# Attention scores in bursts of four blocks, with the high x high products as pairs of 64-row matmuls

## The chip, the cores and the metric

The kernel runs on one core of a Trainium2 chip. The metric is the device time of one execution, in microseconds; of the kernel before it is 1637.64 us, the median of three runs (1636.85 to 1638.16). A smaller time is better.

## What is computed

Attention without a softmax, followed by two layers of a mixture of experts. Cut to what the change touches:

```python
# B, S, D = 4, 3072, 256; d_qk = 64; inputs fp32, drawn from a normal distribution times 0.1
scores = (1 / S) * np.matmul(z, z.transpose(0, 2, 1))     # z: 4 x 3072 x 64
attn = np.maximum(scores, 0.0) ** 2
out = u * np.matmul(attn, v)                              # u, v: 4 x 3072 x 256
# then out.reshape(12288, 256) goes through two layers of 8 experts with 1024 hidden units,
# the first with a capacity of 1536 tokens an expert, the second with 384
```

## The kernel before

Products are made to nearly fp32 exactness out of fp32r matmuls: each operand is split into a high part (a copy in fp32r) and a low part (what is left), and a product is a sum of partial products of highs and lows.

Attention takes the 4 batches in chunks of 512 queries: 6 chunks a batch, 24 in all (`c`, of `NC`). For each chunk it goes through the 24 blocks of 128 keys (`k`, of `KT`); a step `s` is one block of one chunk, 576 in all (`NS`). What a step makes is transposed: keys on partitions, queries on columns.

- `load_z`, `part_z`, `turn_z` bring a tile of 512 rows of z and turn it, so that its 64 features stand on partitions, twice: rows 0 to 63 and again 64 to 127. `turn_z` makes `zHL`: the high part in the upper 64 rows, the low part in the lower. `swap_z` makes `zLH` for one chunk, the same with halves exchanged, by two DMAs from POOL's queue.
- `scores(s)` (lines 363 to 382) makes one block: the first matmul (L368) takes 128 columns of `zHL` as weights and the chunk's `zHL` as moving operand, which gives high x high + low x low; the second (L369) takes the same weights and `zLH`, for the two mixed terms. Both use all 128 rows of the array and 512 columns. ScalarE applies Relu and the scale (L371, `r`). The square `a` is made by VectorE (L379) or ScalarE (L377), its high part `aH` by ScalarE (L376, L380), its low part `aL` by VectorE (L382).
- `av(s)` multiplies with v: for each half `h` of the 256 columns of v three matmuls (L397 to L399) of 128 rows and 512 columns add to the accumulator `accs[h]`, through all 24 blocks. At the last block VectorE multiplies with the turned u (L401, `times_u` in the change) into `xT`.

The order on every queue is that in which the program text issues (nothing is rescheduled). `scores` runs three steps ahead of `av` (`LA`), so TensorE's stream is: two score matmuls of step s + 3, six matmuls of step s, and so on. What else belongs to a chunk hangs on steps as hooks (`at(step, function, ...)`), issued after that step: loading and turning u (`turn_u`, steps 12 and 16 of a chunk), `swap_z` for the next chunk (step 13), and for the chunk before it the gate's logits (`part_x`, `logits`, `turn_l`, `put_l`) and the output (`put_x` at step 9, which for the first ten chunks turns `xT` into `rowb` and issues eight DMAs). In the chunk that ends a batch, and a little ahead, z and v of the next batch are split (`turn_z`, `part_v`). During the last batch the routing of the first expert layer (`prep`, `prep2`) is worked off between the steps. Behind attention come the experts, in `fast`, with 384 to 432 columns a matmul or 256.

PSUM has eight banks: three `acc`, two `sc`, and one each of `mi`, `rt` and `px`.

## Time and profile before

| | |
|---|---|
| median of the runs | 1637.64 us |
| the profiled execution | 1636.56 us, its span 1634.8 us |
| TensorE busy | 1580.8 us, 97% |
| VectorE busy | 1186.5 us, 73% |
| ScalarE busy | 1116.7 us, 68% |
| granted TensorE clock, mean | 0.983 of full speed |
| attention's matmuls | 7.4 to about 1105 us |

Engines are named as in the trace: PE is TensorE, PEld its weight loads, DVE is VectorE, ACT is ScalarE, POOL is GpSimd, SP issues DMAs. A row of a matmul shows 0.39 us for 512 columns although the next one starts 0.23 us later: matmuls are pipelined, and a row contains its way through the array. So lengths of a stream of matmuls are read from their starts. "Issue" as the reason of a gap means that the profile shows nothing that the engine waited for.

### The profile page before, as it was taken

Reading aid. Unit: us, or ns where it says so; the run is one execution under the profiler, and the core shown is the slowest. Engines: PE = TensorE matmul, PEld = TensorE weight load, DVE = VectorE, ACT = ScalarE, POOL = GpSimd, SP = SyncE. Lnnn points to the kernel's source line nnn. Section 1 sums busy time; section 2 is a strip of 40 time slices with the busy share of each in tenths; the row PEclk is TensorE's granted clock in tenths of the full one; section 3 lists DMA queues with packets and bytes.
Section 4 is the critical chain, followed back from the end, with each engine's and each line's share of the span. In section 5 each row is a group of like instructions: output and inputs, shape, how many; then the busy total and the mean of one; then the engine's idle time right before and its main releaser. Section 6 shows DMA issues by size and latency. Waiting matters only on the chain.

```text
span 1634.8 us, 24914 instructions
## 1 busy us (share of the span) xinstructions
PE 1580.8 (97%) x8570; PEld 1326.7 (81%) x8570; DVE 1186.5 (73%) x2338; ACT 1116.7 (68%) x1937; POOL 333.1 (20%) x518
## 2 busy tenths in 40 slices
PE   8999999999999999999999999999999969989997
PEld 5888887888888888888887777878888759978997
DVE  6877788777778767777877877677777766775652
ACT  7877788777788877778987767884444316644552
POOL 1000000000000000000000478642333113323341
PEclk9999999999999999999999999999999969999999
DMA  6111355322335212224310112223343204644540
GB/s 136 20 27 33 68 136 133 73 70 76 72 67 130 76 46 59 59 66 86 77 33 21 28 20 45 60 80 118 101 124 103 84 19 134 189 134 124 153 129 28
DMA packets 282681, 132.44 MB, mean 81 GB/s; under 512 B 216717, under 2 KB 268173, under 8 KB 282544
## 3 DMA queue, kind: packets, MB, share of 16 engines
q1 hardware_dynamic: 269264, 106.90, 26.0%
q0 software_dynamic: 13280, 23.85, 5.0%
q8 instruction: 69, 1.13, 0.3%
q14 instruction: 68, 0.56, 0.1%
HBM read 84.61 MB, written 40.55 MB: 77 GB/s over the span
## 4 chain that ended last, share of the span: by engine, by line
PE 70%; issue 16%; DVE 7%; POOL 2%; ACT 2%; DMA 1%; SPq 1%; POOLq 0%; DVEq 0%
PE acc L397 12%; PE acc L398 12%; PE acc L399 12%; PE sc L1013 9%; PE sc L368 6%; PE sc L369 6%; PE acc L1163 5%; PE mi L1114 2%; DVE pL L225 1%; PE rt L866 1%; PE mi L336 1%; PE acc L1320 1%; PE acc L1321 1%; PE acc L1322 1%; DVE hL L1023 1%
## 5 line engine op out<-in xcount | busy, mean ns | idle before, releaser
L382 DVE TENSOR_TENSOR aL<-a,aH 128x512 fp32r<-128x512 f32 x576 | 398.6, 693 | 212.9 <-ACT a L377 157.8
L371 ACT ACTIVATE r<-sc 128x512 f32<-128x512 f32 x576 | 343.0, 595 | 186.6 <-PE sc L369 180.7
L397 PE MATMUL acc<-aH,pH 128*128 128x512 f32 x1152 | 449.7, 390 | 0.0
L398 PE MATMUL acc<-aL,pH 128*128 128x512 f32 x1152 | 449.0, 390 | 0.0
L399 PE MATMUL acc<-aH,pL 128*128 128x512 f32 x1152 | 448.5, 389 | 0.0
L379 DVE TENSOR_TENSOR a<-r 128x512 f32<-128x512 f32 x344 | 238.5, 693 | 43.0 <-ACT r L371 41.8
L397 PEld LDWEIGHTS acc<-aH,pH 128*128 128x128 f32 x1152 | 216.7, 188 | 45.6
L399 PEld LDWEIGHTS acc<-aH,pL 128*128 128x128 f32 x1152 | 216.7, 188 | 45.6
L398 PEld LDWEIGHTS acc<-aL,pH 128*128 128x128 f32 x1152 | 216.7, 188 | 45.5
L368 PE MATMUL sc<-zHL 128*128 128x512 f32 x576 | 229.8, 399 | 6.3 <-DVE zHL L280 6.0
L1021 ACT ACTIVATE hH<-sc 128x432 fp32r<-128x432 f32 (+2 forms) x192 | 90.0, 469 | 212.5 <-PE sc L1013 208.2
L369 PE MATMUL sc<-zLH,zHL 128*128 128x512 f32 x576 | 225.3, 391 | 0.2 <-DVE zLH L284 0.2
L380 ACT ACTIVATE aH<-r 128x512 fp32r<-128x512 f32 x344 | 217.8, 633 | 10.9
L347 POOL TENSOR_TENSOR lgs<-lgb 32x128 f32<-32x128 f32 x23 | 15.2, 659 | 853.2 <-DVE lgb L344 853.2
L376 ACT ACTIVATE aH<-r 128x512 fp32r<-128x512 f32 x232 | 146.7, 632 | 7.4
L1023 DVE SCALAR_TENSOR_TENSOR hL<-sc,hH 128x432 fp32r<-128x432 f32 (+2 forms) x192 | 99.3, 523 | 65.6 <-ACT hH L1021 65.4
L377 ACT ACTIVATE a<-r 128x512 f32<-128x512 f32 x232 | 142.8, 616 | 0.0
L368 PEld LDWEIGHTS sc<-zHL 128*128 128x128 f32 x576 | 108.7, 189 | 36.1 <-DVE zHL L280 7.4
L1013 PE MATMUL sc<-xTH,pH 128*128 128x384 f32 (+2 forms) x368 | 125.9, 342 | 5.9 <-DVE hL L1023 5.8
L369 PEld LDWEIGHTS sc<-zLH,zHL 128*128 128x128 f32 x576 | 108.8, 189 | 21.5 <-DVE zLH L284 0.5
L1013 PE MATMUL sc<-xTL,pH 128*128 128x384 f32 (+2 forms) x368 | 120.0, 326 | 0.0
L1013 PE MATMUL sc<-xTH,pL 128*128 128x384 f32 (+2 forms) x368 | 119.8, 326 | 0.0
(333 smaller groups left out, 2261.4 us busy)
## 6 DMA issues: line engine op xcount, KB each, us to landing
raw<-in_moe_w_dram SPq DMA_DIRECT2D x84, 512.0 KB, 3.7
raw<-in_v_dram SPq DMA_DIRECT2D x24, 512.0 KB, 4.3
uraw<-in_u_dram SPq DMA_DIRECT2D x192, 64.0 KB, 2.3
out_dram<-zt SPq DMA_DIRECT2D x24, 512.0 KB, 4.2
xb<-xT SPq DMA_DIRECT2D x14, 512.0 KB, 3.4
zr<-in_z_dram SPq DMA_DIRECT2D x96, 64.0 KB, 2.4
zLH<-zHL POOLq DMA_DIRECT2D x46, 128.0 KB, 2.3
ya<-zt SPq DMA_DIRECT2D x10, 544.0 KB, 3.5
```

Of the source, the lines that this page charges most:

```text
L368: nc.tensor.matmul(p, lw, zHL[b, c % QC], start=True, stop=False)
L369: nc.tensor.matmul(p, lw, zLH[c], start=False, stop=True)
L371: nc.scalar.activation(r, p, AF.Relu, scale=SCALE)
L376: nc.scalar.activation(HS[s], r, AF.Square)
L377: nc.scalar.activation(a, r, AF.Square)
L379: nc.vector.tensor_tensor(a, r, r, OP.mult)
L380: nc.scalar.activation(HS[s], r, AF.Square)
L382: nc.vector.tensor_tensor(LS[s], a, HS[s].bitcast(F32), OP.subtract)
L397: nc.tensor.matmul(accs[h], vh[sl], HS[s], start=k == 0, stop=False)
L398: nc.tensor.matmul(accs[h], vh[sl], LS[s], start=False, stop=False)
L399: nc.tensor.matmul(accs[h], vl[sl], HS[s], start=False, stop=k == KT - 1)
L1013: nc.tensor.matmul(p, a, b[:, d, :w], start=i == 0, stop=i == 5)
```

## The change

- Tiles of z are kept in a new form, `zK`: in columns 0 to 255 the high part is in the upper 64 rows and the low part in the lower, in columns 256 to 511 the other way round. For the current chunk there are whole tiles `zHL` and `zLH`. `swap_z` and `copy_z` make these from `zK`: the half columns that stand the right way round are copied by ScalarE, the others exchanged by four DMAs from POOL's queue instead of two.
- `burst(s)` makes the scores of four blocks at once into four banks. First four matmuls of 64 rows for the high x high terms, in the order block 0, 2, 1, 3, of which the first and third use the upper 64 rows of the array (tile position 0) and the second and fourth the lower (tile position 64). Then one matmul of 128 rows a block for both mixed terms. The product low x low is no longer made.
- A burst is issued at the first step of a group of four, for the group after it; `squares` spreads its Relus and squares over the four steps of the group. ScalarE squares for `a` in one or two blocks of four, where before it was every second or every third block.
- `av` takes one half at a time, with the low part of the square in the third matmul instead of the second. In a chunk's last four blocks, the last three are done first for half 0, then for half 1, so that `times_u` of half 0 stands ahead of the matmuls of half 1. At a chunk's first step the burst stands between the halves.
- PSUM in attention: two `acc`, four `sc`, one `mi`, one `rt`, no `px`; after attention a new pool with the layout of before (`open_psum`). The routing's table `tabh` goes to `rt`.
- SBUF: `rowb` shares the one buffer of `uT`, `lgb` the two of `zT`; `r` has three buffers. The constant `idr` is dropped. In the start `turn_z` of the second z tile stands ahead of the first steps.

```diff
...
-        self.ps = pool("ps", 1, space=PSUM)
+        self.nacc, self.nsc = 2, 4
...
-        return self.ps.tile([128, 512], F32, name=name, tag="acc", bufs=3)
+        return self.ps.tile([128, 512], F32, name=name, tag="acc", bufs=self.nacc)
...
-        return self.ps.tile([128, 512], F32, name=name, tag="sc", bufs=2)
+        return self.ps.tile([128, 512], F32, name=name, tag="sc", bufs=self.nsc)
...
-        o = pool.tile([128, 2, 512], F32, name="rowb", bufs=1)
+        o = pool.tile([128, 2, 512], F32, name="rowb", tag="uT", bufs=1)
...
-        with self.tc.tile_pool(name="attn", bufs=2) as W:
+        with self.tc.tile_pool(name="attn", bufs=2) as W, \
+                self.tc.tile_pool(name="psa", bufs=1, space=PSUM) as self.ps:
             return self._attention(W, *args)
+    def open_psum(self):
+        self.ps = self.ctx.enter_context(self.tc.tile_pool(name="ps", bufs=1, space=PSUM))
+        self.nacc, self.nsc = 3, 2
...
+        def parts_z(t, z, o, a, b):
+            nc.vector.tensor_tensor(t[o:o + 64, a:b], z[o:o + 64, a:b], t[o:o + 64, a:b].bitcast(F32), OP.subtract)
...
-            t = zHL[b, i] = W.tile([128, 512], FR, name="zHL", bufs=QC + 2)
-            first = b == i == 0
+            t = zK[b, i] = W.tile([128, 512], FR, name="zK", bufs=QC + 2)
             nc.scalar.activation(t, zT[b, i], AF.Copy)
-            nc.vector.tensor_tensor(t[64:128], zT[b, i][64:128], t[64:128].bitcast(F32), OP.subtract)
-            if first:
-                l = zLH[0] = W.tile([128, 512], FR, name="zLH", bufs=2)
-                nc.scalar.activation(l, zT[b, i], AF.Copy)
-                nc.vector.tensor_tensor(l[0:64], zT[b, i][0:64], l[0:64].bitcast(F32), OP.subtract)
+            if b == i == 0:
+                zHL[0] = W.tile([128, 512], FR, name="zHL", bufs=2)
+                nc.scalar.activation(zHL[0], zT[b, i], AF.Copy)
+                zLH[0] = W.tile([128, 512], FR, name="zLH", bufs=2)
+                nc.scalar.activation(zLH[0], zT[b, i], AF.Copy)
+            parts_z(t, zT[b, i], 64, 0, 256)
+            if b == i == 0:
+                parts_z(zLH[0], zT[b, i], 0, 0, 512)
+            parts_z(t, zT[b, i], 0, 256, 512)
+            if b == i == 0:
+                parts_z(zHL[0], zT[b, i], 64, 0, 512)
...
             b, q = divmod(c, QC)
-            t = W.tile([128, 512], FR, name="zLH", bufs=2)
-            s = zHL[b, q]
-            nc.gpsimd.dma_start(t[0:64], s[64:128])
-            nc.gpsimd.dma_start(t[64:128], s[0:64])
-            zLH[c] = t
+            s = zK[b, q]
+            h = zHL[c] = W.tile([128, 512], FR, name="zHL", bufs=2)
+            l = zLH[c] = W.tile([128, 512], FR, name="zLH", bufs=2)
+            for t, a in ((l, 0), (h, 256)):
+                for o in (0, 64):
+                    nc.gpsimd.dma_start(t[o:o + 64, a:a + 256], s[64 - o:128 - o, a:a + 256])
+        def copy_z(c, d):
+            b, q = divmod(c, QC)
+            t, a = ((zHL[c], 0), (zLH[c], 256))[d]
+            nc.scalar.activation(t[:, a:a + 256], zK[b, q][:, a:a + 256], AF.Copy)
...
-                uT[c] = W.tile([128, 2, 512], F32, name="uT", bufs=1)
+                uT[c] = W.tile([128, 2, 512], F32, name="uT", tag="uT", bufs=1)
...
-                b = W.tile([32, 512], F32, name="lgb", bufs=1)
+                b = W.tile([128, 512], F32, name="lgb", tag="zT", bufs=2)[:32]
...
-        HS, LS = {}, {}
-        LA = 3
-        def scores(s):
+        HS, LS, R = {}, {}, {}
+        GB = 4
+        accs = None
+        def burst(s):
             c, k = divmod(s, KT)
-            b = c // QC
-            p = self.sc()
-            lw = zHL[b, k // 4][:, k % 4 * 128:(k % 4 + 1) * 128]
-            nc.tensor.matmul(p, lw, zHL[b, c % QC], start=True, stop=False)
-            nc.tensor.matmul(p, lw, zLH[c], start=False, stop=True)
-            r = W.tile([128, 512], F32, name="r", bufs=2)
-            nc.scalar.activation(r, p, AF.Relu, scale=SCALE)
+            K = zK[c // QC, k // 4]
+            P = [self.sc() for _ in range(GB)]
+            cols = [slice(j * 128, (j + 1) * 128) for j in range(GB)]
+            for j in (0, 1):
+                nc.tensor.matmul(P[j], K[0:64, cols[j]], zHL[c][0:64], start=True, stop=False, tile_position=(0, 0))
+                nc.tensor.matmul(P[j + 2], K[64:128, cols[j + 2]], zLH[c][64:128], start=True, stop=False,
+                                 tile_position=(64, 0))
+            for j in range(GB):
+                nc.tensor.matmul(P[j], K[:, cols[j]], (zLH if j < 2 else zHL)[c], start=False, stop=True)
+            return P
+        def relu(s, p):
+            R[s] = W.tile([128, 512], F32, name="r", bufs=3)
+            nc.scalar.activation(R[s], p, AF.Relu, scale=SCALE)
+        def square(s, act):
+            r = R.pop(s)
             a = W.tile([128, 512], F32, name="a", bufs=2)
-            HS[s] = W.tile([128, 512], FR, name="aH", bufs=LA + 1)
...
-            if k % (2 if c == 0 or c % QC == QC - 1 or b == B - 1 else 3) == 1:
-                nc.scalar.activation(HS[s], r, AF.Square)
+            h = HS[s] = W.tile([128, 512], FR, name="aH", bufs=GB)
+            if not act:
+                nc.vector.tensor_tensor(a, r, r, OP.mult)
+            nc.scalar.activation(h, r, AF.Square)
+            if act:
                 nc.scalar.activation(a, r, AF.Square)
-            else:
-                nc.vector.tensor_tensor(a, r, r, OP.mult)
-                nc.scalar.activation(HS[s], r, AF.Square)
-            LS[s] = W.tile([128, 512], FR, name="aL", bufs=LA + 1)
-            nc.vector.tensor_tensor(LS[s], a, HS[s].bitcast(F32), OP.subtract)
-        accs = None
-        def av(s):
+            LS[s] = W.tile([128, 512], FR, name="aL", bufs=GB)
+            nc.vector.tensor_tensor(LS[s], a, h.bitcast(F32), OP.subtract)
...
+        def squares(s, j, P):
+            c, k = divmod(s, KT)
+            if j == 0:
+                relu(s, P[0])
+            if j < 3:
+                relu(s + j + 1, P[j + 1])
+            busy = c == 0 or c % QC == QC - 1 or c // QC == B - 1
+            square(s + j, j == 1 or j == 3 and (busy or k // GB % 2 == 1))
+        def av(s, h):
+            c, k = divmod(s, KT)
+            vh, vl = V[c // QC, k // 4]
+            sl = (slice(None), k % 4, slice(h * 128, (h + 1) * 128))
+            nc.tensor.matmul(accs[h], vh[sl], HS[s], start=k == 0, stop=False)
+            nc.tensor.matmul(accs[h], vl[sl], HS[s], start=False, stop=False)
+            nc.tensor.matmul(accs[h], vh[sl], LS[s], start=False, stop=k == KT - 1)
+        def times_u(c, h):
+            nc.vector.tensor_tensor(xT[c][:, h], accs[h], uT[c][:, h], OP.mult)
+        def step(s):
             nonlocal accs
             c, k = divmod(s, KT)
-            b = c // QC
+            j = k % GB
+            g = s - j + GB
+            last = k >= KT - GB
             if k == 0:
                 accs = [self.acc(), self.acc()]
-            vh, vl = V[b, k // 4]
-            if k == KT - 1:
                 xT[c] = self.w.tile([128, 2, 512], F32, name="xT", bufs=1)
-            for h in range(2):
-                sl = (slice(None), k % 4, slice(h * 128, (h + 1) * 128))
-                nc.tensor.matmul(accs[h], vh[sl], HS[s], start=k == 0, stop=False)
-                nc.tensor.matmul(accs[h], vh[sl], LS[s], start=False, stop=False)
-                nc.tensor.matmul(accs[h], vl[sl], HS[s], start=False, stop=k == KT - 1)
-                if k == KT - 1:
-                    nc.vector.tensor_tensor(xT[c][:, h], accs[h], uT[c][:, h], OP.mult)
-                    if h == 0 and s + LA < NS:
-                        scores(s + LA)
+            if j == 0:
+                av(s, 0)
+                if k > 0:
+                    av(s, 1)
+                if g < NS:
+                    PS[0] = burst(g)
+                if k == 0:
+                    av(s, 1)
+            elif last and j == 1:
+                for i in range(3):
+                    av(s + i, 0)
+                times_u(c, 0)
+                for i in range(3):
+                    av(s + i, 1)
+            elif not last:
+                av(s, 0)
+                av(s, 1)
+            if g < NS:
+                squares(g, j, PS[0])
+            if last and j == 1:
+                times_u(c, 1)
...
-        part_v(0, 0)
-        part_z(0, 1)
...
-            at(4 * i - 4 - d, turn_z, 0, i)
             if i > 1:
+                at(4 * i - 5 - d, turn_z, 0, i)
                 at(4 * i - 6 - d, part_z, 0, i)
...
                 at(s0 + 17, load_u, c + 1)
-                at(s0 + 13, swap_z, c + 1)
+                at(s0 + 11, swap_z, c + 1)
+                at(s0 + 13, copy_z, c + 1, 0)
+                at(s0 + 15, copy_z, c + 1, 1)
...
-        for s in range(LA):
-            scores(s)
+        PS[0] = burst(0)
+        squares(0, 0, PS[0])
+        part_v(0, 0)
+        for j in range(1, GB):
+            squares(0, j, PS[0])
+            if j == 1:
+                part_z(0, 1)
+                turn_z(0, 1)
         for s in range(NS):
-            if s + LA < NS and s % KT != KT - 1:
-                scores(s + LA)
-            av(s)
...
-        px = self.px("tabh")
+        px = self.rt("tabh")
...
+        m.open_psum()
         fast(ctx, tc, m, moe_w1, moe_w2, moe2_w1, moe2_w2, out, W, rows)
...
```

## Rows read from the trace of the kernel before

**Rows 1.** The page, engines: busy us, share of the span, instructions.
```profile
PE 1580.8 (97%) x8570; PEld 1326.7 (81%) x8570; DVE 1186.5 (73%) x2338; ACT 1116.7 (68%) x1937; POOL 333.1 (20%) x518
```
**Rows 2.** Stretches: length, busy PE, PEld, DVE, ACT, POOL, clock, DMA share, GB/s.
```profile
300.00:400.00 100.00, 100.00 (x443) 82.09 (x442) 73.86 (x112) 77.93 (x132) 4.53 (x9) 1.00 0.33 79
```
**Rows 3.** Waits of PE, whole run: us in total, times, longest.
```profile
PE sc L368 <- DVE zHL L280: 6.0, 3, 2.7
```
**Rows 4.** Timeline of PE in attention: start us, duration us, engine, line, operation.
```profile
600.29 0.39 PE L369 MATMUL sc<-zLH,zHL 128*128 128x512 f32 x1
...
602.34 0.39 PE L368 MATMUL sc<-zHL 128*128 128x512 f32 x1
...
604.16 0.39 PE L368 MATMUL sc<-zHL 128*128 128x512 f32 x1
```
**Rows 5.** Timeline of PE in the experts, around an 8-row matmul.
```profile
1132.58 0.35 PE L1013 MATMUL sc<-xTL,pH 128*128 128x432 f32 x1
1132.87 0.18 PE L871 MATMUL rt<-gO,ones 8*128 8x32 bf16 x1
1132.98 0.46 PE L1163 MATMUL acc<-hH,pH 128*128 128x432 f32 x1
1133.28 0.36 PE L1163 MATMUL acc<-hL,pH 128*128 128x432 f32 x1
1133.48 0.36 PE L1163 MATMUL acc<-hH,pL 128*128 128x432 f32 x1
```
**Rows 6.** Timeline of PEld there; in brackets the idle time before and why.
```profile
1132.86 0.09 PEld L871 LDWEIGHTS <-ones 8*128 8x128 bf16 x1 [0.28 <-issue]
...
1133.28 0.19 PEld L1163 LDWEIGHTS acc<-hH,pL 128*128 128x128 f32 x1
```
**Rows 7.** Groups by form, PEld: busy us, mean ns | idle before, releaser.
```profile
L984 PEld LDWEIGHTS mi<-idf,g 48*128 48x128 f32 x16 | 2.2, 135 | 2.7 <-issue 2.7
```
**Rows 8.** Timeline of PEld, four 16-row loads in a stream of full ones.
```profile
1113.72 0.32 PEld L352 LDWEIGHTS mi<-idf,lgT 16*128 16x128 f32 x4 [0.29 <-issue]
```
**Rows 9.** Timeline of ACT in attention.
```profile
599.53 0.63 ACT L376 ACTIVATE aH<-r 128x512 fp32r<-128x512 f32 x1
600.08 0.62 ACT L377 ACTIVATE a<-r 128x512 f32<-128x512 f32 x1
600.72 0.60 ACT L371 ACTIVATE r<-sc 128x512 f32<-128x512 f32 x1
601.35 0.63 ACT L380 ACTIVATE aH<-r 128x512 fp32r<-128x512 f32 x1
```
**Rows 10.** Stretches: an ordinary chunk, and one that prepares a batch.
```profile
152.20:196.70 44.50, 44.50 (x197) 36.48 (x196) 32.52 (x51) 34.70 (x59) 1.51 (x3) 1.00 0.30 63
...
241.30:286.70 45.40, 45.16 (x197) 36.04 (x196) 39.32 (x59) 40.85 (x71) 1.97 (x3) 1.00 0.57 140
```
**Rows 11.** Groups by form, ACT, 241.3 to 286.7 us.
```profile
L234 ACT ACTIVATE pH<-raw 128x1024 fp32r<-128x1024 f32 x4 | 4.2, 1046 | 0.0
L279 ACT ACTIVATE zHL<-zT 128x512 fp32r<-128x512 f32 x4 | 2.5, 630 | 2.7 <-DVE zT L273 2.7
```
**Rows 12.** Timeline of DVE, second chunk: `rowb` and the next `uT`.
```profile
81.69 1.30 DVE L195 STREAM_TRANSPOSE rowb<-xT 128x512 f32<-128x512 f32 x2
...
87.13 0.70 DVE L315 STREAM_TRANSPOSE uT<-uraw 128x512 f32<-128x512 f32 x1
```
**Rows 13.** Timeline of SP's queue there.
```profile
82.42 4.18 SPq L199 DMA_DIRECT2D xa<-rowb  x8
```
**Rows 14.** The page, DMA issues: count, KB each, us from issue to landing.
```profile
zLH<-zHL POOLq DMA_DIRECT2D x46, 128.0 KB, 2.3
...
xa<-rowb SPq DMA_DIRECT2D x80, 64.0 KB, 1.9
```
**Rows 15.** Timeline of POOL in the last batch.
```profile
1042.31 0.58 POOL L290 DMA_DIRECT2D zLH<-zHL  x1
```
**Rows 16.** The page, groups: busy us, mean ns | idle before, releaser.
```profile
L382 DVE TENSOR_TENSOR aL<-a,aH 128x512 fp32r<-128x512 f32 x576 | 398.6, 693 | 212.9 <-ACT a L377 157.8
```

More of the change, by code (lines that the diff above doesn't have):

```diff
@@ L138, in consts @@
         make_identity(nc, self.idf)
-        self.idr = c.tile([128, 128], FR, name="idr")
-        nc.scalar.activation(self.idr, self.idf, AF.Copy)
         self.wgraw = c.tile([128, 2, 8], F32, name="wgraw")
@@ L257, in _attention @@
         NC = B * QC
-        zr, zT, zHL, vr, V, zLH, uraw, uT, xT, row, xp, lg = ({} for _ in range(12))
+        zr, zT, zK, vr, V, zHL, zLH, uraw, uT, xT, row, xp, lg = ({} for _ in range(13))
         def at(s, f, *a):
@@ L271, in part_z @@
         def part_z(b, i):
-            zT[b, i] = W.tile([128, 512], F32, name="zT", bufs=2)
+            zT[b, i] = W.tile([128, 512], F32, name="zT", tag="zT", bufs=2)
             nc.vector.transpose(zT[b, i], zr[b, i])
+        def parts_z(t, z, o, a, b):
+            nc.vector.tensor_tensor(t[o:o + 64, a:b], z[o:o + 64, a:b], t[o:o + 64, a:b].bitcast(F32), OP.subtract)
         def turn_z(b, i):
-            t = zHL[b, i] = W.tile([128, 512], FR, name="zHL", bufs=QC + 2)
-            first = b == i == 0
+            t = zK[b, i] = W.tile([128, 512], FR, name="zK", bufs=QC + 2)
@@ L405, in put_l @@
+        PS = [None]
         def put_l(c):
@@ L454, in _attention @@
                     at(t + 3, part_v, b + 1, i)
-        for s in range(LA):
-            scores(s)
+        PS[0] = burst(0)
[6 more added lines that the diff above has]
+                turn_z(0, 1)
         for s in range(NS):
-            if s + LA < NS and s % KT != KT - 1:
-                scores(s + LA)
-            av(s)
+            step(s)
             for f, a in hooks.pop(s, []):
```

## The prediction

> **What bounds the kernel now.** I read the page first: TensorE shows 97% of the span busy, the next engine, VectorE, 73% [rows 1]. A busy matmul row overlaps its neighbour, so that share alone proves little; the table by stretches does. In the attention stage, which runs to about 1105 us and holds all that the diff touches but the order of PSUM banks afterwards, TensorE is busy for 100 us of 100, ScalarE for 78 and VectorE for 74, at the granted clock 1.00, 2.4 GHz [rows 2]. The waits of TensorE agree: the longest entry in the whole run is 6.0 us, three waits for the low parts of z in the start [rows 3]. So attention lasts as long as its matmuls follow each other. Their spacing is in the timeline: from the first score matmul of one block to that of the next, eight matmuls of 512 columns, 1.82 us pass, 0.227 us each [rows 4] (a row reads 0.39 us because it overlaps the next). 576 blocks of eight at 0.227 us are 1046 us. What shortens this stream shortens the run; what only moves work off ScalarE or VectorE doesn't, until one of them is late.
>
> **The change on TensorE.** Per four blocks the score part goes from eight full matmuls to four of 64 rows and four full ones; the 24 of the value product stay. The 64-row ones stand in pairs, on row tiles 0 and 64. If a pair takes the time of one, two slots are saved, 2 x 0.227 = 0.454 us a group, and 144 groups give 65 us. That is what the change would bring if nothing else happened.
>
> But the array goes from its full shape to 64-row tiles and back, once each per group, and the trace of before has this step. In the FFN an 8-row matmul (L871) stands in a stream of full ones with 432 columns, spaced 0.195 us (0.20 in the rows, rounded). The full one before it starts at 1132.58; the weight load of the 8-row one starts at 1132.86, 0.28 us later, after 0.28 us of idle that is put down to nothing but "issue" [rows 5, 6]. Ordinarily the next weights start loading when the matmul before starts (1133.28 and 1133.28), hidden under it. Behind the 8-row one the full matmul takes 0.46 us instead of 0.36: its own weights lie open for 0.10 to 0.11 us [rows 5, 6]. From 1132.58 to 1133.28, 0.70 us, stand two matmuls that would take 0.39. The same holds for 48-row fp32 ones, which use a 64-row tile as the change does: 16 of them cost 2.7 us of idle before their weights, 0.17 each, all of it "issue" [rows 7]; and four 16-row ones show 0.29 us [rows 8].
>
> The Trainium skill says the same in general (TensorEngine Tiling (Array Packing), Key Properties): changing the tiling mode, not just the tile, drains TensorE. This speaks against the change, and the trace agrees [rows 5 to 8]; the skill gives no figure, so the sum goes by the rows.
>
> Now the sum for a group, from the start of the last full matmul before the burst to the start of the first full one in it. Before: five slots, 5 x 0.227 = 1.135 us. After: 0.28 us as read, and 0.03 more since 512 columns take 0.227 and not 0.195, is 0.31 until the first weights load; x until the first 64-row product can start; 0.227 for its pair; l, by which the second tile lags the first because its weights come second; 0.31 until the full weights load; 0.11 until their matmul starts. 0.31 + x + 0.227 + l + 0.31 + 0.11 = 0.957 + x + l. No row shows weights of 64 rows in fp32r or two row tiles at once. Weights of 128 rows lie open for 0.11 us [rows 5]; those of 16 rows follow one another in (0.32 - 0.14)/3 = 0.06 us, with 0.14 the length of one load on a small row tile [rows 7, 8]. So x lies in 0.06 to 0.11 and l in 0 (both loaded at once) to 0.11. I take x = 0.11, the row of the same type, and l = 0.085, the middle of the two loads: 1.152 us, 0.017 more than before. 144 groups: +2.4 us; with the bounds, -0.118 to +0.042 a group, -17 to +6 us. The two saved slots just about pay the two changes of shape. If a pair's halves don't overlap at all, a group costs 0.31 + 0.11 + 3 x 0.227 + 0.31 + 0.11 = 1.521, +0.386, +56 us; if changes of shape cost nothing here, -65 us.
>
> **What feeds TensorE.** Scores now come four blocks at once, a group ahead. From the start of the first full score matmul to its Relu 0.43 us pass (600.29 to 600.72 in [rows 4, 9]); then two Relus and a square at 0.63 each [rows 9] and the subtraction at 0.69 [rows 16] give the first aL 2.6 us after. It is needed 4 + 18 + 2 matmuls later, 24 x 0.227 - 0.43 = 5.0 us. Slack: 2.4 us. With two squares more on ScalarE (0.55 after a square, and the next Relu 0.64 after it [rows 9]) a busy group takes it 4 x 0.63 + 2 x 0.63 + 2 x 0.55 + 2 x 0.64 = 6.2 us of 7.3, so in most chunks it idles a tenth of the time or more (34.7 of 44.5 us before [rows 10]; after, one square and two half copies more, some 36).
>
> Only a chunk that prepares the next batch is tight: 40.9 us of 45.4 [rows 10]. There each group also splits one z tile (0.63) and one v tile (1.05) [rows 11], 7.9 us against 7.3; over five groups that is 3 us too much, with part_x (two more copies of 0.63) and the new half copies (two, each between half of 0.63 and the whole) some 5 us, against 2.4 of slack and what idles around. I take 1 us of stall in each of three such chunks, and 1 us in the first chunk, which splits all of batch 0: +4 us, bounds 0 and +12. VectorE has the same work but a few smaller subtractions; its cover is the quarter of its time that is free.
>
> **Waits and queues.** (1) uT and rowb share one buffer. rowb is turned at 81.69 us, its eight stores are issued from 82.42 for 4.18 us and land 1.9 us after each issue, so until about 88; uT is turned at 87.13 [rows 12 to 14]. turn_u will therefore hold VectorE for about 1 us in ten chunks; queued behind it are the next aL and a, on which the value product waits. Their slack is the 2.4 us above, so I cost it at 0; without that cover 10 us. (2) Only two acc banks: the first matmul of a chunk waits for times_u on half 0. That was finished nine matmuls (2.0 us) earlier, more than the 0.69 us of a VectorE operation of this size [rows 16]: 0, or 24 x 0.7 = 17 us without cover. (3) aH has four buffers, and with halves apart the second block's is free only 12 matmuls after the burst, 1 us after ScalarE wants it, once a chunk: covered by its idle time, else 24 us. (4) POOL issues four swap DMAs a chunk instead of two, at 0.6 us each; they are needed nine steps, 16 us, later, and land in 2.3 us [rows 14, 15]: 0 even among the scatters of the last batch, up to 2 us if these come later for it. lgb in zT's buffers, tabh in rt's bank and the new PSUM pool after attention: 0, bound 2 us. (5) Start: TensorE waits 6.0 us in all for z's tiles, 2.7 at the longest [rows 3]. Now three copies and four subtractions stand before the first mixed term, but z's second tile is turned earlier: 0, plus or minus 2.
>
> **Sum.** +2.4 + 4 = +6.4 us on the profiled execution, 1636.6 us (span 1634.8 and 1.8 around it), 1643.0. The median of the runs lies 1.1 above that execution: 1644.1. I forecast 1644, about 0.4% slower: the order of the work is new and its length is not.
>
> **Rivals.**
> *A. The second tile's weights load with the first's, and little stalls* (faster). Then l = 0 and x = 0.06, -0.118 a group, -17 us: 1620.6. Cheaper changes of shape in a stream of long matmuls would take it on towards 1572, where all 65 us stay. For it: 8-row loads are shorter than 128-row ones. Against it: three kinds of rows show the open weights and the drain alike [rows 5 to 8]. It decides as soon as l is under 0.04 and nothing stalls. The Trainium skill bears on this (TensorE: Matmul & The Clock Gate, Part 3, The mechanism): weight loads for another row group may be pulled ahead and matmuls on row tiles start some 4 ns apart. No row here has two tiles at once; by it the time is this rival's.
> *B. The pairs run one after the other.* The change then doesn't do what it says: +56 us, and 4 of stalls, 1697. For it: no row of before shows two at once, and matmuls start in order. Against it: they use different rows and different banks.
> *C. ScalarE becomes the bound in every chunk* through the held aH buffer and the shared uT buffer: some 1.1 us in each of 24 chunks instead of the 4 us, +26 + 2: 1666. For it: batches of four need four Relus at once. Against it: a fifth of ScalarE's time is idle in most chunks [rows 10].
>
> **How the numbers follow.** Forecast (1630 to 1658) 0.55, A 0.25, B 0.10, C 0.10. About 0.2%, 3.3 us, is what a measurement can tell from no change. Of the forecast's 0.55 some 0.08 fall below 1634.4, 0.13 within 3.3 us of 1637.6, 0.34 above. Faster: 0.25 + 0.08 = 0.33; same 0.13; slower 0.34 + 0.10 + 0.10 = 0.54. The range leaves out B and the far end of A: 1612 to 1668.
>
> **What would show it.** In the changed kernel: two idle stretches per group at the weight loads, before the first 64-row one and before the first full one; starts of the two halves of a pair under 0.11 us apart (0.227 apart would be B); 1.13 to 1.18 us from the last full matmul before a burst to the first full one in it (1.02 would be A); waits of TensorE for aL or aH in the chunks that prepare a batch, and hardly elsewhere. The forecast is wrong if the drains are shorter than the rows of L871 and L984, or if TensorE waits in every chunk.

## The result, and the profile after

The changed kernel takes 1655.53 us, the median of four runs (1654.26 to 1657.11), beside 1637.9 us for the kernel before: 1.0108 times as long, with a 95% interval of 1.009 to 1.0125. It is 17.6 us slower where 6.4 were forecast. The profiled execution has a span of 1653.4 us, 18.6 more than before.

The page, engines of the changed kernel (busy us, share of the span, instructions), which answers [rows 1]:

```profile
PE 1584.9 (96%) x8568; PEld 1253.5 (76%) x8570; DVE 1172.1 (71%) x2349; ACT 1056.4 (64%) x1997; POOL 353.4 (21%) x564
```

Hardly anything shows: TensorE is 4 us busier and GpSimd 20, the others are less busy. So I laid the ends of the chunks beside each other: the start of the second multiplication by u of a chunk (L401 before, L433 after, 24 of them, on VectorE's timeline), us.

| end of chunk | before | after | difference |
|---|---|---|---|
| 0 | 63.66 | 62.39 | -1.27 |
| 4 | 241.32 | 240.50 | -0.82 |
| 5 (prepares a batch) | 286.68 | 287.29 | +0.61 |
| 11 | 553.52 | 554.04 | +0.52 |
| 17 | 820.36 | 820.82 | +0.46 |
| 20 | 968.71 | 969.74 | +1.03 |
| 21 | 1017.72 | 1025.86 | +8.14 |
| 23 | 1106.43 | 1119.37 | +12.94 |
| first expert product | 1106.23 | 1120.72 | +14.49 |
| last matmul | 1622.58 | 1637.14 | +14.56 |
| end of the span | 1634.75 | 1653.37 | +18.62 |

Three batches, 18 of 24 chunks, come out even. 12.5 us come in the six chunks of the last batch, 1.5 in the handover to the experts, nothing in the experts, and 4.1 behind the last matmul. The stretches agree (length, busy PE, PEld, DVE, ACT, POOL, clock, DMA share, GB/s): of the changed kernel a chunk that prepares a batch and an ordinary one, which answer [rows 10], and its last batch in two halves; last, the same two halves of the kernel before.

```profile
240.50:287.30 46.80, 46.03 (x198) 33.28 (x196) 40.51 (x64) 39.65 (x75) 2.65 (x5) 1.00 0.63 153
152.20:196.70 44.50, 44.50 (x198) 33.34 (x198) 31.32 (x50) 32.17 (x62) 2.77 (x5) 1.00 0.25 41
...
820.80:969.70 148.90, 145.57 (x761) 106.03 (x760) 109.66 (x206) 101.51 (x193) 43.07 (x72) 0.99 0.14 28
969.70:1119.40 149.70, 142.16 (x626) 103.22 (x624) 100.58 (x203) 101.92 (x190) 93.82 (x157) 0.99 0.21 53
...
820.40:968.70 148.30, 146.57 (x770) 116.13 (x769) 112.56 (x208) 110.27 (x188) 47.66 (x74) 1.00 0.13 28
968.70:1106.40 137.70, 137.18 (x614) 109.22 (x614) 98.85 (x199) 108.75 (x183) 89.13 (x145) 1.00 0.23 57
```

In the ordinary chunk TensorE is busy throughout, as before; in the last batch it stands still for 3.3 and 7.5 us, where before it was 1.7 and 0.5. What it waits for there (us in total, times, longest), 820 to 1121 us of the changed kernel:

```profile
PE tabh L656 <- DVE tL L651: 3.0, 2, 1.7
PE rt L605 <- DVE pre L570: 2.7, 3, 1.9
PE rt L563 <- DVE hM L718: 1.8, 2, 1.6
PE sc L1082 <- DVE st L867: 1.4, 1, 1.4
PE mi L1053 <- DVE pL L1057: 1.1, 1, 1.1
PE rt L775 <- DVE mm L772: 1.1, 1, 1.1
PE rt L569 <- DVE cs L564: 1.0, 2, 0.6
```

and from 820 to 1107 us of the kernel before:

```profile
PE tabh L587 <- DVE tL L582: 1.3, 1, 1.3
PE rt L494 <- DVE hM L649: 0.5, 1, 0.5
PE rt L706 <- DVE mm L703: 0.4, 1, 0.4
```

These are not the products of attention. All but two are the small products of the first layer's routing, which is worked off a step at a time between the blocks of the last batch; each waits for a tile (tL, pre, hM, cs, mm) that VectorE makes shortly before it. The two with pL and st belong to the start of the experts, and the one with st lies in the handover. One such wait in the timeline of the changed kernel:

```profile
954.87 0.63 ACT L408 ACTIVATE aH<-r 128x512 fp32r<-128x512 f32 x1 [1.27 <-PE acc L429]
...
955.98 0.39 PE L430 MATMUL acc<-aL,pH 128*128 128x512 f32 x1
956.06 1.34 DVE L412 TENSOR_TENSOR aL<-a,aH 128x512 fp32r<-128x512 f32 x1 [1.36 <-ACT a L410]
...
957.32 0.68 DVE L651 TENSOR_TENSOR tL<-io,clo 128x1024 bf16<-128x1024 bf16 x1
...
958.05 1.62 PE L656 MATMUL tabh<-tR,tL 128*128 128x96 bf16 x8 [1.68 <-DVE tL L651]
959.37 0.78 PE L428 MATMUL acc<-aH,pH 128*128 128x512 f32 x1
959.94 0.63 PE L429 MATMUL acc<-aH,pL 128*128 128x512 f32 x1
960.37 0.63 PE L430 MATMUL acc<-aL,pH 128*128 128x512 f32 x1
960.80 0.63 PE L428 MATMUL acc<-aH,pH 128*128 128x512 f32 x1
```

TensorE is through with the block at 956.4. VectorE has tL, which the routing's product needs, behind an aL of the next group, and that aL waited 1.36 us for ScalarE, whose aH had itself waited for TensorE to read the old one; its row is then 1.34 us long where 0.69 is usual (1.17 ahead of the next such wait), and why stays open. The aL is wanted a group later, the tL at once. Behind the wait the matmuls stand 0.43 us apart instead of 0.227: the granted clock is at its lower level, 1.2 GHz, for 3.4 us from 958.4, and again from 982.3 behind the next wait for tL, of 1.3 us. Not every such wait was followed by that: the one of 1.6 us for hM, at 994.0, and the longest, 1.9 us for pre at 1103.5, were not. Two stretches of the changed kernel, the clock third from the end:

```profile
955.00:965.00 10.00, 8.32 (x35) 5.95 (x34) 4.79 (x7) 3.52 (x7) 8.70 (x15) 0.83 0.35 54
...
990.00:1000.00 10.00, 8.12 (x37) 5.60 (x36) 5.86 (x15) 5.80 (x12) 7.12 (x14) 1.00 0.19 58
```

By the spacing of the matmuls the two stretches at 1.2 GHz cost 1.1 and 1.6 us (in the first of them the small products of the routing took as long as at full clock, 1.3 us). Waits of 10.8 us in the last batch against 2.2 before, and 2.7 for the clock: 8.6 + 2.7 = 11.3 of the 12.5. Where the other 1.2 lie is not worked out.

The burst itself, which answers [rows 4 to 6]:

```profile
598.44 0.39 PE L430 MATMUL acc<-aL,pH 128*128 128x512 f32 x1
598.76 0.49 PE L390 MATMUL sc<-zHL,zK 64*128 64x512 f32 x1
598.76 0.49 PE L391 MATMUL sc<-zLH,zK 64*128 64x512 f32 x1
599.10 0.39 PE L390 MATMUL sc<-zHL,zK 64*128 64x512 f32 x1
599.10 0.39 PE L391 MATMUL sc<-zLH,zK 64*128 64x512 f32 x1
599.42 0.73 PE L394 MATMUL sc<-zLH,zK 128*128 128x512 f32 x2
599.99 0.63 PE L394 MATMUL sc<-zHL,zK 128*128 128x512 f32 x2
600.46 0.39 PE L428 MATMUL acc<-aH,pH 128*128 128x512 f32 x1
```

and its weight loads:

```profile
598.76 0.18 PEld L390 LDWEIGHTS sc<-zHL,zK 64*128 64x128 f32 x1 [0.35 <-issue]
598.76 0.18 PEld L391 LDWEIGHTS sc<-zLH,zK 64*128 64x128 f32 x1
...
599.42 0.30 PEld L394 LDWEIGHTS sc<-zLH,zK 128*128 128x128 f32 x2 [0.36 <-issue]
```

Both halves of a pair load their weights and start within the 10 ns that the rows resolve; ahead of the first pair and ahead of the first full product the weights start 0.32 us after the matmul before, with the idle time put down to "issue". From 598.44 to 600.46 are 2.02 us, where nine products before (one of the value product, eight of scores) took 9 x 0.227 = 2.04.

### The profile page after: what moved, and what is told of

It reads as the page before. It is cut to its first block, busy times and chain, and to the rows that moved or that the text cites. A ratio compares the mean times of both kernels' runs of the same rounds, so it can differ in the third digit from the quotient of the medians.

```text
span 1653.4 us, 25385 instructions
## 1 busy us (share of the span) xinstructions
PE 1584.9 (96%) x8568; PEld 1253.5 (76%) x8570; DVE 1172.1 (71%) x2349; ACT 1056.4 (64%) x1997; POOL 353.4 (21%) x564
## 3 DMA queue, kind: packets, MB, share of 16 engines
q0 software_dynamic: 16960, 23.85, 5.3%
q8 instruction: 69, 1.13, 0.3%
## 4 chain that ended last, share of the span: by engine, by line
PE 82%; DVE 9%; issue 4%; ACT 3%; POOL 1%; DMA 1%; SPq 0%; DVEq 0%; POOLq 0%; ACTq 0%
PE acc L428 15%; PE acc L429 15%; PE acc L430 14%; PE sc L394 9%; PE sc L1082 9%; PE sc L390 5%; PE acc L1232 5%; PE mi L1183 2%; DVE pL L223 1%; PE mi L356 1%; PE rt L935 1%; DVE aL L412 1%; PE acc L1390 1%; PE acc L1391 1%; PE acc L1389 1%
## 5 line engine op out<-in xcount | busy, mean ns | idle before, releaser
L428 PE MATMUL acc<-aH,pH 128*128 128x512 f32 x1152 | 454.4, 394 | 0.2 <-ACT pH L232 0.2
L399 ACT ACTIVATE r<-sc 128x512 f32<-128x512 f32 x576 | 328.6, 597 | 169.1 <-PE sc L394 168.7
L407 DVE TENSOR_TENSOR a<-r 128x512 f32<-128x512 f32 x330 | 224.9, 682 | 93.0 <-ACT r L399 92.7
L410 ACT ACTIVATE a<-r 128x512 f32<-128x512 f32 x246 | 154.0, 626 | 0.7 <-DVE aL L412 0.7
L390 PE MATMUL sc<-zHL,zK 64*128 64x512 f32 x288 | 105.5, 445 | 5.1 <-ACT zK L286 4.2
L705 POOL DMA_INDIRECT tt<-TP,hidx x92 | 97.8, 1063 | 51.9 <-DVE ntail L725 26.1
L391 PE MATMUL sc<-zLH,zK 64*128 64x512 f32 x288 | 106.4, 446 | 0.3 <-ACT r L399 0.3
L394 PE MATMUL sc<-zLH,zK 128*128 128x512 f32 x288 | 105.9, 449 | 0.0
L223 DVE TENSOR_TENSOR pL<-raw,pH 128x1024 fp32r<-128x1024 f32 x80 | 97.5, 1219 | 10.7 <-ACT pH L218 10.6
```

Source lines behind the costliest of these rows:

```text
L223: self.nc.vector.tensor_tensor(l, raw, h.bitcast(F32), OP.subtract)
L390: nc.tensor.matmul(P[j], K[0:64, cols[j]], zHL[c][0:64], start=True, stop=False, tile_position=(0, 0))
L394: nc.tensor.matmul(P[j], K[:, cols[j]], (zLH if j < 2 else zHL)[c], start=False, stop=True)
L399: nc.scalar.activation(R[s], p, AF.Relu, scale=SCALE)
L407: nc.vector.tensor_tensor(a, r, r, OP.mult)
L410: nc.scalar.activation(a, r, AF.Square)
```

## The experiments

Three theories on the time lost: (1) the routing's products wait because VectorE's and ScalarE's queues hold the squares of the next group ahead of what feeds them, be it for the order alone (1b) or because these squares wait for a buffer of aH (1a); (2) they wait because the table tabh lost its own PSUM bank; (3) the 4.1 us at the end come from GpSimd's closing drain. On the burst the question is whether its two changes of shape cost what the two saved slots bring.

A word on how to read the times. The first ten runs fell on three other chips, on which ScalarE and VectorE stop for up to 16 us at a time between the end of chunk 20 and the experts, in kernels of either kind. In the run steps_first, on ScalarE's timeline:

```profile
1058.69 0.61 ACT L410 ACTIVATE a<-r 128x512 f32<-128x512 f32 x1
1069.48 1.08 ACT L399 ACTIVATE r<-sc 128x512 f32<-128x512 f32 x2 [10.18 <-remote]
```

"remote" means that no row shows what released it; the scores that it reads had been there since 1056. The kernel before takes 1658.8 to 1663.2 us on these chips. So from these ten runs I use what lies ahead of the stops (ends of chunks up to 20), the drain at the end, and totals only roughly. The last two runs were on a chip without them.

**The lost bank, alone.** In the kernel before:

```diff
-        px = self.px("tabh")
+        px = self.rt("tabh")
```

> The kernel before with one edit: the slot table tabh is built in the bank rt instead of its own bank px. Nothing is left out. Theory 1 (squares ahead of the routing's operations): no change, 1636.4 to 1639.4 us. Theory 2 (the lost bank makes the routing wait): 5 us or more slower, 1643 to 1652 us, with waits of TensorE at tabh or at the next product into rt.

Measured: 1661.48 us beside 1663.18, 0.9996 (0.9979 to 1.0014), where theory 2 asked for 5 us or more; up to chunk 19 its chunk ends keep a constant 2.37 to 2.40 us from those of the kernel before. So the bank alone makes no wait in the kernel before; that it makes none in the changed one is shown further down, where the waits go although tabh stays in rt. Theory 2 falls.

**Four exchanging transfers instead of two, alone.** In the kernel before:

```diff
-            nc.gpsimd.dma_start(t[0:64], s[64:128])
-            nc.gpsimd.dma_start(t[64:128], s[0:64])
+            for a in (0, 256):
+                for o in (0, 64):
+                    nc.gpsimd.dma_start(t[o:o + 64, a:a + 256], s[64 - o:128 - o, a:a + 256])
```

> The kernel before with one edit: the exchange of the two halves of z for the next chunk is issued as four transfers of half the columns instead of two (46 transfers more on GpSimd's software queue over the kernel, the same bytes). Nothing is left out. Theory 3 (the closing drain of GpSimd grows with what went through its software queue): the last drain is 7 us or more instead of 3.8, and the time 3 to 4 us longer, 1641 to 1642 us. Rival (the longer drain of the changed kernel is due to something else, such as the spacing of the last scatters): drain 3.8 us, 1636.5 to 1639.3 us.

GpSimd's drains on the last lines (shortest/median/longest ns), in the kernel before, in the changed one, and in this one:

```profile
L1601 POOLq DRAIN  x3: 46/107/3831, 1629.7 to 1634.1; - x3
```

```profile
L1671 POOLq DRAIN  x3: 46/107/7342, 1645.2 to 1653.1; - x3
```

```profile
L1602 POOLq DRAIN  x3: 46/107/7342, 1668.8 to 1676.7; - x3
```

The drain is that of the changed kernel to the nanosecond, and this edit alone makes it: theory 3 holds, for 3.5 of the 4.1 us behind the last matmul. The total, 1675.05 beside 1663.18 us (1.007), has stops in it and says no more.

**No exchanging transfer on GpSimd.** In the kernel before, the two are issued with `nc.sync.dma_start`:

> The kernel before with one edit: its two transfers that exchange the halves of z are issued from SyncE's queue instead of GpSimd's software queue (46 fewer on the latter). Nothing is left out. Theory 3 (the closing drain of GpSimd follows from what went through its software queue): the drain is shorter than 3.8 us, 1 to 3.5 us off the time (0.998 to 0.9995 of the kernel before). Rival: drain 3.8 us as before and no change.

The drain is 1.14 us. Up to chunk 19 its chunk ends keep a constant 0.48 to 0.49 us from those of the kernel before, so SyncE's queue carries the transfers for nothing. The total is 1683.05 beside 1658.79 us (1.0147), where 0.998 to 0.9995 was expected: chunk 21 is 21.4 us longer than in the kernel before and chunk 22 another 23.6, with stops of 35 us in sum on ScalarE. Why they are more here than in the kernel before stays open.

**Full products in the burst.** Every high x high product is made over all 128 rows, so low x low is in the scores again:

```diff
-                nc.tensor.matmul(P[j], K[0:64, cols[j]], zHL[c][0:64], start=True, stop=False, tile_position=(0, 0))
-                nc.tensor.matmul(P[j + 2], K[64:128, cols[j + 2]], zLH[c][64:128], start=True, stop=False,
-                                 tile_position=(64, 0))
+                nc.tensor.matmul(P[j], K[:, cols[j]], zHL[c], start=True, stop=False)
+                nc.tensor.matmul(P[j + 2], K[:, cols[j + 2]], zLH[c], start=True, stop=False)
```

> The changed kernel with the four high x high products of a burst made as whole 128-row products of the same two tiles (they then hold low x low too, which the changed kernel leaves out); order, banks, buffers and transfers stay. Per group of four blocks this puts two product slots back (2 x 0.227 us) and takes the two changes of array shape away. By the rows of the changed kernel (burst to next whole product 2.02 us against 9 x 0.227 = 2.041) it is 0.02 us per group slower, +3 us over 144 groups: 1657 to 1660 us. By the sum of the prediction (a group 0.017 us dearer than before) it is 2.4 us faster: 1653. If the loss against the kernel before came from the half-array products themselves, the time would fall by 10 us or more, to 1645 or less.

**Two half bursts.** The full products of a pair follow it at once:

```diff
+                for i in (j, j + 2):
+                    nc.tensor.matmul(P[i], K[:, cols[i]], (zLH if i < 2 else zHL)[c], start=False, stop=True)
-            for j in range(GB):
-                nc.tensor.matmul(P[j], K[:, cols[j]], (zLH if j < 2 else zHL)[c], start=False, stop=True)
```

> The changed kernel with one edit: the burst of a group is made as two half bursts, each one pair of half-array products and then its two whole ones, so TensorE changes its shape four times a group instead of twice. Nothing is left out. By the rows of the changed kernel (1.09 us from the last whole product before two pairs to the first whole one behind them, 0.24 to 0.34 us of it the second pair): a half burst has 0.75 to 0.85 us in place of 1.09/2, so a group is 0.18 to 0.38 us longer, a chunk 1.1 to 2.3 us, the time 26 to 55 us more than the changed kernel. Rival (the change of shape itself is free, the price lies in the pairs): no more than 3 us.

Both are read from the three ordinary chunks from the end of chunk 12 to that of 15. Before: 44.473 us a chunk (597.99 to 731.41). After: 44.413. Full products: 44.497 (604.63 to 738.12). Half bursts: 47.013 (630.51 to 771.55). With six groups a chunk, one more round trip of the shape costs (47.013 - 44.413)/6 = 0.433 us; two slots less one round trip are worth (44.497 - 44.413)/6 = 0.014, which makes the round trip 0.454 - 0.014 = 0.440. Two ways, one price. The half bursts in the timeline:

```profile
630.50 0.39 PE L430 MATMUL acc<-aL,pH 128*128 128x512 f32 x1
630.82 0.50 PE L390 MATMUL sc<-zHL,zK 64*128 64x512 f32 x1
...
631.25 0.50 PE L394 MATMUL sc<-zLH,zK 128*128 128x512 f32 x1
631.59 0.40 PE L394 MATMUL sc<-zHL,zK 128*128 128x512 f32 x1
631.91 0.49 PE L390 MATMUL sc<-zHL,zK 64*128 64x512 f32 x1
```

The 0.32 us ahead of a changed shape stand there twice as often. The totals of full products and half bursts are 1693.6 us (1.0201 of the kernel before) and 1734.63 us (1.0442), stops included. By the chunks the full products cost 0.014 x 144 = 2 us more than the changed kernel (3 expected), so the rival by which the half products themselves make the loss falls. The half bursts cost 0.433 x 144 = 62 us, more than the 26 to 55 expected. The full products tell something on theory 1 too: between the ends of chunks 17 and 20 TensorE waits 1.9 us for tL, 1.1 for mm and 0.6 for cs in this run as well, so these waits come with the new order and not with the pairs.

**Routing steps ahead of the squares.** In this version of the changed kernel the main loop issues, for each step, the products, then the routing's step, then the squares (`rest` is the end of `step`, from `if g < NS`) and the hooks:

```diff
             step(s)
-            for f, a in hooks.pop(s, []):
-                f(*a)
             for s0, p, c in stages:
                 ...
+            rest(s)
+            for f, a in hooks.pop(s, []):
+                f(*a)
```

> The changed kernel with one edit of order: in each step of attention the routing's step is issued ahead of the squares of the group four blocks ahead, so that VectorE and ScalarE meet the routing's operations first. Nothing is left out. Theory 1 (the routing's small products wait because the squares stand ahead of the operations that feed them): the routing waits of TensorE between 820 and 1121 us fall from some 12 us to 3 or less, the granted clock stays at 1.00 there, the first expert product comes 9 to 12 us earlier than the 1120.7 us of the changed kernel, and the time falls from 1655.5 to 1644 to 1648 us. Theory 2 (the routing waits because the table of slots lost its own bank): no more than 2 us change, 1653 to 1657 us. If the second products of attention had no slack for squares that come a routing step later, new waits of TensorE on a (aH, aL) would appear in the last batch and the time would stay or rise.

1677.26 beside 1663.18 us (1.0092), with the stops shown above, where 1644 to 1648 was expected. Ahead of them, from the end of chunk 17 to that of 20, it took 144.5 us with 0.14 us of waits, the changed kernel 148.9 with 3.3. So it was run once more, beside the changed kernel on one chip:

> The changed kernel once more, only as the yardstick for the run beside it on the same chip. Nothing is left out. Expected: routing waits of TensorE of 3.3 to 3.6 us between the ends of chunks 17 and 20, as in its two other profiles.

> The kernel of the run steps_first (routing steps ahead of the squares) on the same chip as the changed kernel. Nothing is left out. Theory 1b (order in the queues): 8 to 12 us faster than the changed kernel beside it, and less than 0.5 us of routing waits between the ends of chunks 17 and 20, which lie 4 to 5 us closer together than in the changed kernel. Rival (the gain there is given back by the squares that then come late, as new waits of TensorE on aH or aL, or by longer unexplained stops): within 3 us of it.

1641.94 us (1640.99 to 1643.46), the changed kernel beside it 1655.65 and the kernel before 1637.82: 13.7 us less than the changed kernel (8 to 12 expected), 1.0027 (1.0017 to 1.0037) of the kernel before. The changed kernel's waits over chunks 18 to 20 are 3.3 us here too. Its last batch in the same two stretches, and all that TensorE waits for from 820 to 1110 us:

```profile
821.40:965.90 144.50, 144.34 (x762) 105.28 (x761) 112.50 (x208) 101.65 (x193) 46.12 (x74) 1.00 0.14 29
965.90:1107.10 141.20, 139.43 (x625) 101.71 (x623) 100.19 (x201) 101.66 (x190) 96.21 (x156) 1.00 0.22 56
```

```profile
PE sc L1087 <- DVE st L872: 1.4, 1, 1.4
PE mi L1058 <- DVE pL L1062: 1.2, 1, 1.2
PE rt L610 <- DVE pre L575: 0.5, 1, 0.5
```

The waits for tL, hM, mm and cs are gone, the clock stays at 1.00, the batch takes 285.7 us where the changed kernel took 298.6 and the kernel before 286.1. Theory 1 holds: the place in the queues makes the waits. The edit also puts the routing's step ahead of the hooks of that step (u, the gate's logits, the output), so how much of the 13.7 us the squares alone account for is not measured. What is left against the kernel before is 4.1 us: the closing drain (7.34 us here too) makes 3.5, the wait for st in the handover 1.4, and the last batch is 0.4 shorter.

**A fifth buffer for aH.** The wait above began with aH's buffer, so it could be the buffer and not the order:

```diff
-            h = HS[s] = W.tile([128, 512], FR, name="aH", bufs=GB)
+            h = HS[s] = W.tile([128, 512], FR, name="aH", bufs=GB + 1)
```

> The changed kernel with one edit: five buffers instead of four for aH (the order of the queues stays, the squares ahead of the routing's operations). Nothing is left out. Theory 1a (the squares of a step wait for the buffer that the same step's second products read last, so they and the routing's operation behind them are late by aH's 0.63 us and aL's 0.69): with the fifth buffer ScalarE no longer waits for TensorE's last reading of aH, the routing waits of TensorE between 820 and 1121 us fall from some 12 us to 6 or less, and the ends of chunks 18 to 20 come 1 to 3 us earlier than in the changed kernel (0.5 to 2 us before the kernel before instead of 0.1 to 1.1 behind it). Theory 1b (only the order in the queues counts, the buffer does not): the chunk ends stay within 0.7 us of the changed kernel and the routing waits at 9 us or more. Where the two engines stop for reasons that no row shows (ends of chunks 21 to 23 in the other runs of such a chip) only the chunks ahead of that are compared.

ScalarE's waits for that buffer, ahead of the stops, fall from 23.9 us in the changed kernel (820.8 to 969.7, the first row) to 2.7 here (818 to 968, the second):

```profile
ACT aH L408 <- PE acc L429: 23.9, 24, 4.9
...
ACT aH L408 <- PE acc L429: 2.7, 5, 0.8
```

TensorE's do not:

```profile
PE tabh L656 <- DVE tL L651: 2.7, 2, 1.9
PE rt L775 <- DVE mm L772: 1.1, 1, 1.1
PE rt L569 <- DVE cs L564: 0.6, 1, 0.6
```

4.4 us here, 3.3 in the changed kernel over the same three chunks. The ends of chunks 18 to 20 do come 1.3 to 2.8 us before the changed kernel's, as theory 1a expected, but so does the end of chunk 17, by 2.8: the lead is older than these waits, and the three chunks take 150.5 us where the changed kernel took 148.9. The buffer's share, theory 1a, falls; the order is what counts. (1678.58 beside 1659.31 us.)

**Order and SyncE's queue together.** Two versions, without and with the fifth buffer, were to show whether the change can beat the kernel before; the changed kernel ran beside the first:

> The changed kernel itself, run again beside the kernel before on the same chip, as the yardstick for the runs beside it. Nothing is left out. Expected 1.0108 times the kernel before (interval so far 1.009 to 1.0125), a closing drain of GpSimd of 7.3 us, and routing waits of TensorE of some 12 us between 820 and 1121 us.

> The changed kernel with two edits: each routing step is issued ahead of the squares, and the four transfers that exchange the halves of z are issued from SyncE's queue instead of GpSimd's software queue. Nothing is left out. Theories 1 and 3 together: against the changed kernel the routing waits go (9 to 12 us) and the closing drain shrinks from 7.3 us to 3.8 us or less (4 us or more), so 13 to 17 us faster than the changed kernel, that is 0.998 to 1.003 of the kernel before; by the chunk ends of the run steps_first (2.5 to 4.2 us earlier than before at the ends of chunks 20 and 21) and a drain of 3.8 us or less it is 0.996 to 0.999. If SyncE's queue is held up by transfers that wait for zK, the loads of u and the puts of x behind them come late and chunks grow beyond 44.4 us.

> The changed kernel with three edits together: routing steps ahead of the squares, five buffers for aH, and the four exchanging transfers on SyncE's queue. Nothing is left out. Theories 1 and 3: ends of chunks 18 to 20 2 to 5 us before those of the kernel before, a closing drain of 1.1 us instead of 3.8, so on a chip without the unexplained stops 0.995 to 0.999 of the kernel before; with them, as in the runs so far, 1.005 to 1.018.

1684.2 us (1.0152) and 1687.33 (1.0175), the changed kernel 1686.12 (1.0156 where 1.0108 was expected): where the stops are, the 13 to 17 us expected of the first version do not show; the ends of chunk 23 come 39 to 48 us behind those of the kernel before in the table. Ahead of the stops, at the end of chunk 19, the first stands 1.45 and the second 2.43 us before the kernel before, but 1.44 and 1.73 of that are there since chunk 1. The drain is 1.14 us in both. On a chip without stops neither was run, so whether they beat the kernel before is open.

## Why the prediction was right in sign and short in size

*What bounds the kernel.* Right: in an ordinary chunk TensorE is busy 44.50 of 44.50 us, and the time is the length of its stream.

*The burst.* Forecast +0.017 us a group, measured -0.020 by the rows and (44.413 - 44.473)/6 = -0.010 by the chunks: -1.4 us in all instead of +2.4. The term that was mis-sized is l, the lag of the second tile: taken as 0.085, measured 0. x is 0.10 by the first pair's rows of 0.49 us instead of 0.39 (taken 0.11), the two drains are 0.32 each (taken 0.31). From the last full product to the first full one in the burst that makes 0.98 us to its weights and 0.11 for these, 1.09, between the 1.13 to 1.18 of the forecast and the 1.02 of rival A. From there to the value product are 0.93 us for four slots of 0.227, 0.02 more than the sum had. That l is 0 was rival A's condition; its 0.06 for x, which it needed for 1620.6, did not come. Both halves' weights load at once and both products start at once, so rival B falls too. The Trainium skill (TensorE: Matmul & The Clock Gate, Part 3, The mechanism) states that weights for another row group are pulled ahead of matmuls in flight and that matmuls on different row tiles start about 4 ns apart. The trace agrees, as far as rows of 10 ns show it.

*Stalls.* Forecast 4 us in the chunks that prepare a batch and the first. Chunk 5 is 1.4 us longer (1.7 and 2.6 in two more profiles of the changed kernel), chunks 11 and 17 0.4 each; by the end of chunk 1 the start has given 0.5 back. To the end of chunk 17 the sum is +0.5 where 2.4 x 18/24 + 4 = 5.8 were forecast.

*Waits (1) to (3)* at nothing: right, between 20 and 820 us TensorE's waits in attention show one of 0.4 us for an aL and one of 0.3 for a bank of sc besides z's tiles and the gate; rival C with its 1.1 us in every chunk falls. *tabh in rt's bank*, 0 with a bound of 2: right.

*Wait (4)* at 0, up to 2: wrong. I asked whether the four transfers land in time, and they do; I did not follow GpSimd's queue to its end, where the drain grows by 3.5 us.

*The step that failed* is "What feeds TensorE", which left the routing's waits out of the sum. It counted the squares' slack for the product with v, 2.4 us, and rightly found it enough. It never asked who stands behind the squares: in the last batch VectorE also makes hM, cs, pre, tL and mm, and TensorE wants each within the step. Exchanging the order is worth 13.7 us where 17.6 were lost; that is shown. Why the same order cost only 2.2 us of waits before is argued: then TensorE had two score products and six others in every step, now it runs through three steps of a group without scores while VectorE's work stays spread over four, and so it arrives early at the routing's products. So the sign was right by luck: the terms that were to make the kernel slower came to about nothing (+0.5 us to the end of chunk 17), and the loss lies in things that stood in no term, the routing's waits with the clock behind two of them (12.5 us with the rest of the last batch), the handover (1.5) and GpSimd's drain (3.5).

## What to carry to other kernels

When work is gathered into bursts on one engine, go through every consumer on the other engines' queues, not only the one that the bursts feed: a result that is wanted in the same step must be issued ahead of one that is wanted a group later, and that exchange of order was worth 13.7 us here. A change of array shape there and back cost 0.44 us, about two slots of 512 columns, so two pairs a burst only pay for it. What was added to GpSimd's software queue was paid at the end of the program, 3.5 us here, so look at the closing drain.

## What the runs showed of the hardware

- GpSimd's closing drain follows what went through its software queue: 1.136 us with 9600 packets there, 3.831 with 13280, 7.342 with 16960, the same to the nanosecond in every run of a kind. It is not proportional: 46 transfers less took off 2.7 us, 46 more added 3.5.
- Two 64-row products on row tiles 0 and 64 load their weights and run at the same time; a round trip of the shape costs 0.433 to 0.440 us, 0.32 ahead of each changed weight load.
- In the changed kernel two waits of TensorE, of 1.7 and 1.3 us, were followed by 3.4 us at 1.2 GHz, and two others, of 1.6 and 1.9 us, were not; in its run beside `steps_first` it was those of 1.6 us for tL and 1.9 us for pre that were, and the one of 1.3 was not. With the waits gone the clock stayed at 2.4 GHz throughout the last batch.
- On three of the chips ScalarE and VectorE stopped for 3 to 16 us at a time in the last batch, with nothing in the trace that they waited for. How often and how long differed between kernels that differ only in a few transfers. The cause is open.
